# Attention's product with v turned round: queries in rows, the weights' sum as a 65th column, division on VectorE

## The chip, the core and the metric

The kernel runs on one NeuronCore of a Trainium2 chip. Its engines work side by side, each through its own queue in order: TensorE (PE) multiplies matrices, VectorE (DVE), ScalarE (ACT) and GpSimd (POOL) do elementwise work, SyncE (SP) issues the DMA transfers. Matmuls write to PSUM, eight banks of 2 KB per partition. The metric is the device time of one execution in microseconds (us), as the median of three runs.

## What is computed

Causal attention with a decay in the scores (4 batches, 8 heads, 576 positions, 64 columns), then a two-matrix layer with a leaky ReLU (512 to 2048 to 512), then a second layer (512 to 1024, softmax gate, layer norm, back to 512). The change touches only the middle of the attention:

```python
scores = scores - np.max(scores, axis=-1, keepdims=True)
attn = np.exp(scores)
attn = attn / (np.sum(attn, axis=-1, keepdims=True) + 1e-09)
return np.matmul(attn, v).astype(np.float32)
```

## The kernel before

Two heads make a pair, and there are 16 pairs, four to a batch. Queries are cut into blocks of 128 rows; blocks 0 to 3 are whole, block 4 holds the last 64 rows of both heads at once. `pair` (L765) runs one pair. The first four pairs run in two halves: blocks 0 and 1 from a float32 tile `qa` without splitting, later blocks 2 to 4; the other twelve run whole. For each unit of blocks `scores` (L675) lets PE write the scores into PSUM banks `ps_s` (four of them), DVE subtracts the mask and takes the row's extreme (L693), then `softmax` (L636) does the rest: ACT computes exp in place and gives the row's sum as a second output, its accumulator (L643), an engine of choice adds the small guard (L650), DVE takes the reciprocal (L661), ACT or DVE writes the normalised weight's high float16 half to `hl` (L665), DVE the low half (L669), and `turn` (L672) lets a DMA transpose both into `pt`, keys in partitions.

`pv` (L736) then multiplies: the stationary operand is v of 128 keys, split by `prep_v` (L594) into 64 high and 64 low columns side by side in `VT`, and the moving operand is 128 queries of `pt`. High and low half of the weights take one matmul each:

```python
mm(ps.t[:, 128 * i:128 * i + 128], vl(p, hd, j), pts[i][0].t[:, pts[i][1] + k * (i + 1) + j, :],
   j == 0 and k == 0, j == i and k == 1)
```

The output stands with v's columns in partitions, the layout that the next layer wants. Its two halves are added up in `evac` (L721): ACT copies the low one to `xr` (L725), DVE adds the high one (L728). There is one bank `ps_v`. `pv4` (L750) does the same for block 4 with 64 moving columns. `xr` goes out to `xs_d` by DMA, and the FFN reads it back as tokens.

The FFN's first part (`ffn_a`, L875) works in nine blocks of 256 tokens with nine of sixteen chunks of weights; a token block needs the four pairs of its batch. Its matmuls fill PE between attention matmuls. The second part (`ffn_b`, `layer2`) follows.

The order on every engine is not written by hand. `Plan.run` (L163) is a list scheduler: every operation has a priority and an assumed duration, buffers come from tags with a fixed number of tiles, and an operation that may run on several engines (`copy_f`, `sub_f`, `flex`) takes the one that the planner finds cheapest then. Attention comes before FFN on PE. Its constants are the same before and after.

## Time and profile before

| | |
|---|---|
| median of 3 runs | 850.2 us (849.22 to 850.39) |
| the profiled execution's own time | 849.04 us |
| its span in the profile | 847.2 us |
| busy share of the span | PE 92%, DVE 62%, ACT 58%, POOL 43% |
| mean granted clock of PE | 0.98 |
| DMA queue q1 | 105.67 MB, 52.3% of the 16 engines' span |

The span is what the profile shows from the first to the last instruction; the execution's own time has some 2 us more around it. A stretch of the span can have another limit than the whole, so it is read stretch by stretch. "Idle before" in a group of instructions is the time that the engine waited ahead of them, with the releaser.

### The profile page before, as it was taken

The numbers are of one execution on the slowest core, as the hardware profiler recorded it, in microseconds if no ns is written. First come the engines' busy times: TensorE is split into PE (matmuls) and PEld (weight loads), VectorE is DVE, ScalarE is ACT, GpSimd is POOL, SyncE is SP. The second block draws the span as 40 slices with busy tenths as digits, with TensorE's granted clock in tenths as the row PEclk, the third lists the DMA queues.
The fourth block names the chain that finished last, engine by engine and source line by source line (L and its number), as shares of the span: only waits on it lengthen the run. The fifth ranks groups of instructions, "written<-read, shape, count | busy, mean of one in ns | idle before, by whom it ended". The sixth has DMA issues, their size and how long they took to land.

```text
span 847.2 us, 15672 instructions
## 1 busy us (share of the span) xinstructions
PE 777.7 (92%) x5648; PEld 707.1 (83%) x5648; DVE 523.0 (62%) x1301; ACT 488.8 (58%) x1210; POOL 364.5 (43%) x433
## 2 busy tenths in 40 slices
...
GB/s 285 199 231 226 178 142 183 129 185 156 184 137 179 126 197 115 147 165 187 168 175 157 190 26 87 71 68 26 87 38 101 26 88 38 87 26 63 26 42 95
DMA packets 179757, 106.66 MB, mean 126 GB/s; under 512 B 146608, under 2 KB 162496, under 8 KB 179680
## 3 DMA queue, kind: packets, MB, share of 16 engines
q1 hardware_dynamic: 179680, 105.67, 52.3%
q8 instruction: 44, 0.72, 0.4%
...
## 4 chain that ended last, share of the span: by engine, by line
PE 58%; DVE 4%; DMA 3%; ACT 3%; issue 1%; POOL 1%; DVEq 0%; SPq 0%; ACTq 0%; POOLq 0%
PE ps_f L470 36%; PE ph L470 11%; PE py L470 8%; DMA pt<-hl 2%; PE ps_s L470 1%; PE ps_v L470 1%; DMA tr<-hl 1%; ACT hl L424 1%; DVE hl L435 1%; DVE st L657 0%; ACT ps_s L643 0%; DVE g L841 0%; DVE raw L952 0%; DVE ps_s L693 0%; DVE s L944 0%
## 5 line engine op out<-in xcount | busy, mean ns | idle before, releaser
L470 PE MATMUL ps_f<-x,wi 128*128 128x256 f32 x972 | 129.6, 288 | 0.8 <-DVE g L841 0.8
L470 PEld LDWEIGHTS ps_f<-x,wi 128*128 128x128 f32 x972 | 123.6, 193 | 2.0 <-DVE g L841 1.2
L470 PE MATMUL ps_f<-g,wo 128*128 128x256 f32 x972 | 124.2, 283 | 1.2 <-DVE g L841 1.2
L470 PEld LDWEIGHTS ps_f<-g,wo 128*128 128x128 f32 x972 | 119.5, 188 | 1.8 <-DVE g L841 1.5
L470 PE MATMUL ps_s<-kq 128*128 128x512 f32 (+4 forms) x352 | 95.4, 396 | 25.8 <-DVE hl L435 22.4
L470 PE MATMUL ps_f<-x,wib 128*128 128x256 f32 x756 | 98.3, 281 | 0.7 <-DVE g L841 0.4
L470 PEld LDWEIGHTS ps_s<-kq 128*128 128x128 f32 x352 | 65.9, 226 | 39.2 <-DVE hl L435 22.2
L470 PE MATMUL ph<-wi,g 128*128 128x512 f32 x408 | 98.3, 396 | 0.0
L839 ACT ACTIVATE g<-ps_f 128x256 fp32r<-128x256 f32 x144 | 55.2, 383 | 71.9 <-PE ps_f L470 70.8
L470 PEld LDWEIGHTS ps_f<-x,wib 128*128 128x128 f32 x756 | 92.8, 188 | 1.8 <-DVE g L841 1.7
L470 PEld LDWEIGHTS ph<-wi,g 128*128 128x128 f32 x408 | 76.0, 188 | 17.6
L439 POOL TENSOR_TENSOR kq<-raw,kq 64x576 fp32r<-64x576 f32 (+2 forms) x55 | 82.6, 1502 | 14.6 <-ACT kq L424 9.2
L435 DVE SCALAR_TENSOR_TENSOR hl<-ps_s,st,hl 128x512 f16<-128x512 f32 (+4 forms) x160 | 82.2, 538 | 9.1 <-ACT hl L424 7.3
L643 ACT ACTIVATE ps_s<-ps_s,st 128x512 f32<-128x512 f32 (+4 forms) x160 | 78.8, 493 | 13.0 <-DVE st L693 7.7
L841 DVE TENSOR_TENSOR g<-ps_f,g 128x256 fp32r<-128x256 f32 x144 | 60.2, 420 | 41.0 <-ACT ps_f L840 39.3
L470 PE MATMUL ps_f<-wo,x 128*128 128x512 f32 x348 | 83.9, 396 | 0.0
L424 ACT ACTIVATE hl<-ps_s,st 128x512 f16<-128x512 f32 (+4 forms) x146 | 73.0, 538 | 12.3 <-issue 3.2
L470 PEld LDWEIGHTS ps_f<-wo,x 128*128 128x128 f32 x348 | 64.7, 188 | 14.9
L470 PE MATMUL ps_v<-pt,VT 128*128 128x128 f16 (+1 forms) x928 | 65.4, 234 | 12.7 <-DVE xr L728 4.3
L470 PE MATMUL py<-g,wob 128*128 128x256 f32 x567 | 76.6, 279 | 0.0
L470 PEld LDWEIGHTS <-VT 128*128 128x128 f16 x928 | 56.2, 110 | 22.8 <-issue 13.2
L470 PEld LDWEIGHTS py<-g,wob 128*128 128x128 f32 x567 | 72.4, 188 | 1.9
(152 smaller groups left out, 1198.5 us busy)
## 6 DMA issues: line engine op xcount, KB each, us to landing
...
```

Of the source, the lines that this page charges most:

```text
L424: nc.scalar.activation(o, i, CP, scale=1.0 if scale is None else scale)
L435: nc.vector.scalar_tensor_tensor(o, a, scale, b, op0=ALU.mult, op1=ALU.subtract)
L439: (nc.vector if eng == DVE else nc.gpsimd).tensor_tensor(o, a, b, op=ALU.subtract)
L470: nc.tensor.matmul(o, lhsT=l, rhs=r, start=start, stop=stop)
L643: P.op(ACT, act(W, 1, True) + 93, lambda view=view, j=j, k=k: nc.scalar.activation(view(), view(), AF.Exp, bias=sts.t[:, j:j + 1], scale=- ...
L839: P.op(ACT, act(n, 0, True), lambda: nc.scalar.activation(g.t[:, 0, 0:n], h(), AF.Prelu, scale=WSC, alpha=0.01), eprio, w=[(g, 0)], r=[ps])
L841: P.op(DVE, dve(n) + 60, lambda: nc.vector.tensor_tensor(g.t[:, 1, 0:n], h(), g.t[:, 0, 0:n].bitcast(F32), op=ALU.subtract), eprio, w=[(g, ...
```

## The change

The product with v is turned round. `pt` (128 keys by 128 queries) is now the stationary operand and v the moving one, so that a query stands in a row. `VT` holds per block and head 64 low columns, 64 high ones and a column of ones; high columns and ones together are 65 moving columns, and the 65th output column is the sum of the row's weights. A pair of weight halves and v halves takes four matmuls (`pv_mms`), all into the same 65 columns of PSUM, instead of two of 128 columns. The softmax gives no sums any more: exp has no second output, guard and reciprocal are gone, the halves in `hl` are those of exp times the constant 2^15, and blocks 0 and 1 of one bank are split in one pass of 384 columns. The division comes after the product, on DVE: guard and reciprocal of the 65th columns, then one instruction that scales by `u` and the reciprocal into `xn` (`xn4` for block 4, both heads in one matrix with zeros elsewhere). PE turns `xn` back by a float32 matmul with the identity (`across` for blocks 0 to 3, 128 columns a block; inside `pv4` with `ident2`, 64 columns), and ACT or DVE copies the result to `xr`. `xn` lies in the three tiles `sd` that the decay has done with. `prep_v` writes its unused outputs to tiles of their own.

```diff
-    P.tag("VT", tiles(ap, "VT", NVT, [128, 5, 2, 2, 64], F16))
+    P.tag("VT", tiles(ap, "VT", NVT, [128, 5, 2, 130], F16))
+    P.tag("rs", tiles(ap, "rs", 3, [128, 8], F32))
+    P.tag("xn4", tiles(ap, "xn4", 1, [128, 128], F32))
+    vabs = ap.tile([128, 640], F16, name="vabs")
+    vmin = ap.tile([128, 128], F32, name="vmin")
+    ident2 = ap.tile([128, 64], F32, name="ident2")
...
+    heirs("sd", *[lambda t: [("xn", t[:, 0:512].rearrange("p (a b) -> p a b", a=4))]] * 3)
...
+        nc.vector.tensor_tensor(ident2, one_at[:, 0:64], one_at[:, 64:128], op=ALU.add)
+        for v in P.tags["VT"].free:
+            nc.gpsimd.memset(v[:, :, :, 128:129], 1.0)
+        for x in P.tags["xn4"].free:
+            nc.gpsimd.memset(x, 0.0)
...
-        half = lambda l: v.t[:, :, :, l].rearrange("p j h d -> p (j h) d")
+        half = lambda l: v.t[:, :, :, 64 - 64 * l:128 - 64 * l].rearrange("p j h d -> p (j h) d")
...
-                nc.scalar.activation(v.t.rearrange("p j h l d -> p (j h l d)")[:, 0:640], R(), AF.Abs, accum_out=va.t)
...
+                nc.scalar.activation(vabs, R(), AF.Abs, accum_out=va.t)
...
-            v.t.rearrange("p j h l d -> p (j h l d)")[:, 0:256].bitcast(F32), ps.t[:, 0:128], mask[:, 0:128], -1.0, -(2.0 ** -97),
...
+            vmin, ps.t[:, 0:128], mask[:, 0:128], -1.0, -(2.0 ** -97),
...
-    def softmax(parts, prio):
-
-
-        sts, n, nb = parts[0][1], 0, len(parts)
+    def softmax(sts, parts, groups, prio):
...
         hl, pt = P.buf("hl"), P.buf("pt")
-        one = parts[0][2] == parts[-1][2]
-        for k, (view, _, j, W, pieces, ps) in enumerate(parts):
-            P.op(ACT, act(W, 1, True) + 93, lambda view=view, j=j, k=k: nc.scalar.activation(
-                view(), view(), AF.Exp, bias=sts.t[:, j:j + 1], scale=-1.0, accum_out=sts.t[:, 3 + k:4 + k]), prio,
-                w=[(sts, 2)], rw=[ps], r=[(sts, j)])
-
-        ns = 1 if one else nb
-        total, scale = lambda: sts.t[:, 3:3 + ns], lambda: sts.t[:, 6:6 + ns]
-
-        def guard(e):
-            if one and nb == 2:
-                nc.vector.scalar_tensor_tensor(scale(), total(), 1.0e-9, sts.t[:, 4:5], op0=ALU.add, op1=ALU.add)
-                nc.vector.tensor_scalar(scale(), scale(), PS, None, op0=ALU.mult)
-            elif e == ACT:
-                nc.scalar.activation(scale(), total(), CP, scale=PS, bias=1.0e-9 * PS)
-            else:
-                (nc.vector if e == DVE else nc.gpsimd).tensor_scalar(scale(), total(), 1.0e-9, PS, op0=ALU.add, op1=ALU.mult)
-
-        engs = (DVE,) if one and nb == 2 else REC_ENGS
-        flex(engs, [{ACT: 100.0, DVE: 70.0 * nb, POOL: 165.0}[e] for e in engs], guard, prio, w=[(sts, 3)], r=[(sts, 2)])
-        P.op(DVE, 75, lambda: nc.vector.reciprocal(sts.t[:, 9:9 + ns], scale()), prio, w=[(sts, 4)], r=[(sts, 3)])
-        for view, _, j, W, pieces, ps in parts:
-            rs = lambda j=j: sts.t[:, 9 + j:10 + j]
-            for ho, lo, so, w in pieces:
-                copy_f(lambda ho=ho, w=w: hl.t[:, ho:ho + w], lambda so=so, w=w, view=view: view()[:, so:so + w], w, prio,
-                       engs=HI_ENGS, scale=rs, psum=True, w=[(hl, ho)], r=[ps, (sts, 4)])
-            for ho, lo, so, w in pieces:
-                sub_f(lambda lo=lo, w=w: hl.t[:, lo:lo + w], lambda so=so, w=w, view=view: view()[:, so:so + w],
-                      lambda ho=ho, w=w: hl.t[:, ho:ho + w], w, prio, engs=(DVE,), scale=rs,
-                      w=[(hl, lo)], r=[ps, (sts, 4), (hl, ho)])
-                n += 2 * w
+        for view, j, W, ps in parts:
+            P.op(ACT, act(W, 0, True), lambda view=view, j=j: nc.scalar.activation(
+                view(), view(), AF.Exp, bias=sts.t[:, j:j + 1], scale=-1.0), prio, rw=[ps], r=[(sts, j)])
+        n = 0
+        for view, at, W, ps in groups:
+            copy_f(lambda at=at, W=W: hl.t[:, at:at + W], view, W, prio, engs=HI_ENGS, scale=lambda: 1.0 / PS, psum=True, w=[(hl, at)], r=ps)
+            sub_f(lambda at=at, W=W: hl.t[:, at + W:at + 2 * W], view, lambda at=at, W=W: hl.t[:, at:at + W], W, prio, engs=(DVE,),
+                  scale=lambda: 1.0 / PS, w=[(hl, at + W)], r=ps + [(hl, at)])
+            n += 2 * W
         turn(lambda: pt.t[:, 0:n // 128], lambda: hl.t[:, 0:n], n, prio - 500, w=[pt], r=[hl])
         return pt
...
+            parts.append((view, j, W, key))
+            w = 384 if joint else W
+            chunk[i] = (at // 128 + c0 // 128, at // 128 + (c0 + w) // 128)
+            if not joint or i == 1:
+                groups.append((lambda w=w, ps=ps: ps.t[:, 0:w], at, w, [ps]))
+                at += 2 * w
...
+        pt = softmax(sts, parts, groups, prio)
+        return {i: (pt, *c) for i, c in chunk.items()}
...
-    def evac(p, hd, ps, xr, c0, c1, dst0, prio):
-        n = c1 - c0
-        a, b = 64 * hd, 64 * (1 - hd)
-        u = U[p]
-        P.op(ACT, act(n, 1, True), lambda: nc.scalar.activation(
-            xr.t[a:a + 64, dst0:dst0 + n], ps.t[b:b + 64, c0:c1], CP, scale=u.t[b:b + 64]), prio,
-            w=[(xr, (hd, dst0))], r=[ps, u])
-        P.op(DVE, dve(n) + 60, lambda: nc.vector.scalar_tensor_tensor(
-            xr.t[a:a + 64, dst0:dst0 + n], ps.t[a:a + 64, c0:c1], u.t[a:a + 64],
-            xr.t[a:a + 64, dst0:dst0 + n], op0=ALU.mult, op1=ALU.add), prio, rw=[(xr, (hd, dst0))], r=[ps, u])
...
     def vl(p, hd, j):
 
-        return VT[p].t[:, j, hd].rearrange("p l d -> p (l d)")
-
-    def pv(p, hd, pts, xr, prio):
-        ps, blocks = P.buf("ps_v"), sorted(pts)
-        bufs = {id(b): b for b, _ in pts.values()}
...
+        return v[:, 0:64], v[:, 64:129]
+
+    def pv_mms(o, pair, v, first, last):
+
+        h, l = pair
+        vlo, vhi = v
+        mm(o, h, vhi, first, False)
+        mm(o[:, 0:64], h, vlo, False, False)
+        if l is not None:
+            mm(o[:, 0:64], l, vlo, False, False)
+            mm(o, l, vhi, False, last)
+
+    def pv(p, hd, pts, xn, prio):
+        ps, rs, blocks = P.buf("ps_v"), P.buf("rs"), sorted(pts)
...
+        def pe():
+            for n, i in enumerate(blocks):
+                pt, h, l = pts[i]
+                for j in range(i + 1):
+                    pv_mms(ps.t[:, 65 * n:65 * n + 65], (pt.t[:, h + j], pt.t[:, l + j]), vl(p, hd, j), j == 0, j == i)
+
+        P.op(PE, sum(4 * (i + 1) * mmh(65) for i in blocks), pe, prio, w=[ps], r=[VT[p]] + list(bufs.values()))
+        o = lambda a, b: ps.t[:, 0:65 * nb].rearrange("p (n d) -> p n d", d=65)[:, :, a:b]
+        P.op(DVE, 70, lambda: nc.vector.tensor_scalar(rs.t[:, 0:nb].unsqueeze(2), o(64, 65), 1.0e-9 / PS, None, op0=ALU.add), prio, w=[(rs, 0)], r=[ps])
+        P.op(DVE, 75, lambda: nc.vector.reciprocal(rs.t[:, 4:4 + nb], rs.t[:, 0:nb]), prio, w=[(rs, 1)], r=[(rs, 0)])
+        P.op(DVE, dve(64 * nb) + 60, lambda: nc.vector.scalar_tensor_tensor(
+            xn.t[:, b0 % 4:b0 % 4 + nb, 64 * hd:64 * hd + 64], o(0, 64), U[p].t, rs.t[:, 4:4 + nb].unsqueeze(2).to_broadcast([128, nb, 64]),
+            op0=ALU.mult, op1=ALU.mult), prio, w=[(xn, hd)], r=[ps, (rs, 1), U[p]])
...
+    def pv4(p, pt, xr, prio):
+
+        ps, rs, xn = P.buf("ps_v"), P.buf("rs"), P.buf("xn4")
+
+        def pe():
+            for hd in range(2):
+                o = ps.t[:, 65 * hd:65 * hd + 65]
+                for j in range(4):
+                    pv_mms(o, (pt.t[:, j], pt.t[:, 4 + j]), vl(p, hd, j), j == 0, False)
+                vlo, vhi = vl(p, hd, 4)
+                mm(o[:, 0:64], pt.t[:, 8], vlo, False, False)
+                mm(o, pt.t[:, 8], vhi, False, True)
+
+        P.op(PE, 36 * mmh(65), pe, prio, w=[ps], r=[VT[p], pt])
+        own = [slice(64 * hd, 64 * hd + 64) for hd in range(2)]
+        for hd, a in enumerate(own):
+            P.op(DVE, 70, lambda hd=hd, a=a: nc.vector.tensor_scalar(
+                rs.t[a, 0:1], ps.t[a, 65 * hd + 64:65 * hd + 65], 1.0e-9 / PS, None, op0=ALU.add), prio, w=[(rs, hd)], r=[ps])
+        P.op(DVE, 75, lambda: nc.vector.reciprocal(rs.t[:, 4:5], rs.t[:, 0:1]), prio, w=[(rs, 2)], r=[(rs, 0), (rs, 1)])
+        for hd, a in enumerate(own):
+            P.op(DVE, dve(64) + 60, lambda hd=hd, a=a: nc.vector.tensor_scalar(
+                xn.t[a, a], ps.t[a, 65 * hd:65 * hd + 64], U[p].t[a], rs.t[a, 4:5], op0=ALU.mult, op1=ALU.mult), prio, w=[(xn, hd)], r=[ps, (rs, 2), U[p]])
+        P.op(PE, 107.0, lambda: mm(ps.t[:, 256:320], xn.t, ident2, True, True), prio, rw=[ps], r=[xn], heat=HEAT)
+        copy_f(lambda: xr.t[:, 512:S], lambda: ps.t[:, 256:320], 64, prio, engs=HI_ENGS, psum=True, w=[(xr, 1)], r=[ps])
...
+    def across(p, xn, blocks, xr, prio):
...
         def pe():
             for i in blocks:
-                for j in range(i + 1):
-                    for k in range(2):
-                        mm(ps.t[:, 128 * i:128 * i + 128], vl(p, hd, j), pts[i][0].t[:, pts[i][1] + k * (i + 1) + j, :],
-                           j == 0 and k == 0, j == i and k == 1)
-
-        P.op(PE, sum(2 * (i + 1) * mmh(128) for i in blocks), pe, prio, w=[ps], r=[VT[p]] + list(bufs.values()))
-        evac(p, hd, ps, xr, 128 * blocks[0], 128 * (blocks[-1] + 1), 128 * blocks[0], prio)
...
+                mm(ps.t[:, at(i)], xn.t[:, i], ident.bitcast(F32), True, True)
+
+        P.op(PE, len(blocks) * 215.0, pe, prio, w=[ps], r=[xn], heat=HEAT)
+        a, b = 128 * blocks[0], 128 * blocks[-1] + 128
+        copy_f(lambda: xr.t[:, a:b], lambda: ps.t[:, a:b], b - a, prio, engs=HI_ENGS, psum=True, w=[(xr, 0)], r=[ps])
...
-            pv(p, hd, pts, xr, prio + AV)
+            pv(p, hd, pts, xn, prio + AV)
...
+        across(p, xn, [i for i in blocks if i < 4], xr, prio + AV)
```

In numbers of instructions on PE: 928 products with v become 1856, each with its load of weights, and 64 transposes of 128 and 16 of 64 columns are added. 88 DMA transposes are issued before and after, and SP's queue holds 364 rows both times.

First place, PE, the end of a product with v in one of the first pairs (`VT` is v, `pt` the transposed weights, `sd` a tile that holds `xn`). Before:

```order
L470 LDWEIGHTS VT_106
L470 MATMUL ps_v_164<-pt_131,VT_106 128x128
L470 LDWEIGHTS VT_106
L470 MATMUL ps_v_164<-pt_131,VT_106 128x128
L470 MATMUL ps_s_161<-kq_0_144 128x384
L470 MATMUL ps_s_161<-kq_1_145 128x384
```

Now:

```order
L477 LDWEIGHTS pt_136
L477 MATMUL ps_v_171<-VT_105,pt_136 128x64
L477 LDWEIGHTS pt_136
L477 MATMUL ps_v_171<-VT_105,pt_136 128x64
L477 LDWEIGHTS pt_136
L477 MATMUL ps_v_171<-VT_105,pt_136 128x65
L477 MATMUL ps_s_170<-qa 128x256
L477 MATMUL ps_f_163<-ident,va_142 128x128
L477 MATMUL ps_s_168<-kq_0_151 128x384
L477 MATMUL ps_s_168<-kq_1_152 128x384
L477 MATMUL ps_v_171<-ident,sd_124 128x128 x2
```

Loads come from `pt`, the matmuls are 65 and 64 columns wide, and the turn back stands four matmuls later, behind the DVE work that it needs.

Second place, DVE, within a whole pair (`st` holds row statistics, `rs` the sums and reciprocals; an `ISA` row is the masked extreme or the reading of its result). Before:

```order
L693 ISA st_124 128x1
L435 SCALAR_TENSOR_TENSOR hl_126<-ps_s_161,st_123,hl_126 128x512
L661 RECIPROCAL st_119<-st_119 128x1
L693 ISA ps_s_162,st_124<-ps_s_162,mask 128x384
L693 ISA st_124 128x1
L427 CAST kq_1_141<-kq_0_140 64x640
L435 SCALAR_TENSOR_TENSOR hl_127<-ps_s_160,st_119,hl_127 128x512
L693 ISA ps_s_161,st_121<-ps_s_161,mask 128x512
L693 ISA st_121 128x1
L728 SCALAR_TENSOR_TENSOR xr_132<-ps_v_164,u_110,xr_132 64x512
```

Now:

```order
L687 ISA ps_s_169,st_131<-ps_s_169,mask 128x384
L687 ISA st_131 128x1
L687 ISA ps_s_168,st_128<-ps_s_168,mask 128x512
L687 ISA st_128 128x1
L741 TENSOR_SCALAR rs_110<-ps_v_171 128x4
L687 ISA ps_s_167,st_131<-ps_s_167,mask 128x256
L687 ISA st_131 128x1
L742 RECIPROCAL rs_110<-rs_110 128x4
L442 SCALAR_TENSOR_TENSOR hl_132<-ps_s_169,hl_132 128x384
L743 SCALAR_TENSOR_TENSOR sd_124<-ps_v_171,u_116,rs_110 128x4x64
```

The reciprocal ahead of the low half is gone; three instructions after the product take the place of the merge on L728, with other work between them.

Third place, PE, where FFN blocks fill it (`g`, `wo` are the FFN's operands):

```order
L477 MATMUL ps_f_163<-g_906,wo_72 128x256 x3
L477 MATMUL ps_f_163<-g_907,wo_73 128x256 x3
L477 MATMUL ps_f_163<-g_908,wo_74 128x256 x3
L477 MATMUL ps_f_163<-g_909,wo_75 128x256 x3
L477 MATMUL ps_v_171<-ident,sd_123 128x128 x2
L477 MATMUL ps_f_162<-g_906,wo_72 128x256 x3
L477 MATMUL ps_f_162<-g_907,wo_73 128x256 x3
L477 MATMUL ps_f_162<-g_908,wo_74 128x256 x3
L477 MATMUL ps_f_162<-g_909,wo_75 128x256 x3
L477 LDWEIGHTS pt_136
```

The turn back has twelve matmuls of the FFN ahead of it, between it and the product; before there was no such step.

## Rows read from the trace of the kernel before

**Rows 1.** The page, busy time, share of the span and instructions of each engine.
```profile
PE 777.7 (92%) x5648; PEld 707.1 (83%) x5648; DVE 523.0 (62%) x1301; ACT 488.8 (58%) x1210; POOL 364.5 (43%) x433
```

**Rows 2.** Busy time (instructions) by stretch: PE, weight loads, DVE, ACT, POOL, granted clock, DMA.
```profile
core 0: us, PE busy (x) PEld busy (x) DVE busy (x) ACT busy (x) POOL busy (x), PEclk, DMA share, GB/s
0.00:98.00 98.00, 53.77 (x269) 39.74 (x269) 85.64 (x232) 77.74 (x183) 78.78 (x94) 1.00 0.87 228
98.00:183.00 85.00, 82.52 (x744) 79.12 (x744) 71.14 (x223) 76.39 (x207) 52.06 (x50) 0.96 0.78 159
183.00:219.00 36.00, 24.52 (x168) 20.46 (x168) 29.87 (x91) 26.55 (x71) 21.30 (x22) 0.68 0.79 168
219.00:368.00 149.00, 143.90 (x1342) 137.08 (x1342) 118.32 (x360) 127.69 (x357) 71.39 (x76) 0.98 0.74 148
368.00:847.00 479.00, 472.96 (x3133) 430.67 (x3132) 218.06 (x399) 180.44 (x396) 140.97 (x194) 1.00 0.33 89
```

**Rows 3.** Timeline of PE, 80 to 125 us: start, length, group of instructions.
```profile
84.04 1.65 PE L470 MATMUL ps_v<-pt,VT 128*128 128x128 f16 x14 [0.71 <-ACT hl L424]
85.45 0.99 PE L470 MATMUL ps_s<-kq 128*128 128x384 f32 x2
...
98.08 2.91 PE L470 MATMUL ps_f<-x,wi 128*128 128x256 f32 x12
```

**Rows 4.** Timeline of PE around 219 and 368 us.
```profile
219.05 0.77 PE L470 MATMUL ps_f<-x,wi 128*128 128x256 f32 x2
...
367.84 10.32 PE L470 MATMUL ps_f<-g,wo 128*128 128x256 f32 x84
```

**Rows 5.** Waits of PE, 183 to 219 us: us in total, times, longest.
```profile
PE ps_s L470 <- DVE hl L435: 8.6, 3, 3.8
PE ps_v L470 <- DVE xr L728: 1.8, 1, 1.8
```

**Rows 6.** Timeline of PE, 250 to 262 us: products with v and what follows.
```profile
252.55 1.29 PE L470 MATMUL ps_v<-pt,VT 128*128 128x128 f16 x20
253.65 0.89 PE L470 MATMUL ps_s<-kq 128*128 128x512 f32 x4
...
258.55 0.70 PE L470 MATMUL ps_v<-pt,VT 128*128 128x64 f16 x18 [0.86 <-DMA pt<-hl]
259.08 2.04 PE L470 MATMUL ps_f<-g,wo 128*128 128x256 f32 x15
```

**Rows 7.** Records of one tile, 32.0 to 33.2 us: min/median/max ns, first and last start.
```profile
L470 PE MATMUL ps_s<-qa x4: 634/634/635, 31.7 to 33.0; 66*128 66x256 f32 x4
```

**Rows 8.** Groups by line: weight loads for the products with v; busy us, mean ns.
```profile
L470 PEld LDWEIGHTS <-VT 128*128 128x128 f16 x928 | 56.2, 110 | 22.8 <-issue 13.2 <-DMA pt<-hl 3.9 <-DVE st L693 2.3
```

**Rows 9.** Groups by line and form on DVE and ACT.
```profile
L728 DVE SCALAR_TENSOR_TENSOR xr<-ps_v,u,xr 64x64 f32<-64x64 f32 (+2 forms) x72 | 34.7, 482 | 8.3 <-ACT xr L725 7.0
...
L725 ACT ACTIVATE xr<-ps_v,u 64x64 f32<-64x64 f32 (+2 forms) x72 | 33.8, 470 | 10.5 <-PE ps_v L470 6.4 <-DVE xr L728 2.7
L643 ACT ACTIVATION_READ_ACCUMULATOR ps_s<-ps_s,st 128x1 f32 x160 | 32.4, 203 | 0.2
...
L661 DVE RECIPROCAL st<-st 128x1 f32<-128x1 f32 (+2 forms) x88 | 14.2, 163 | 10.5 <-POOL st L657 6.7 <-ACT st L655 2.4
...
L1000 ACT ACTIVATE ot<-ps_f 128x512 f32<-128x512 f32 x18 | 10.8, 597 | 59.7 <-PE ps_f L470 54.7 <-issue 5.0
...
L652 DVE SCALAR_TENSOR_TENSOR st<-st 128x1 f32<-128x1 f32 x16 | 10.3, 642 | 0.5 <-ACT ps_s L643 0.3
...
L657 DVE TENSOR_SCALAR st<-st 128x1 f32<-128x1 f32 (+2 forms) x18 | 7.4, 410 | 1.7 <-ACT ps_s L643 1.5
...
L424 ACT ACTIVATE hl<-ps_s,st 128x512 f16<-128x512 f32 x48 | 32.9, 685 | 7.6 <-issue 3.2 <-DVE st L661 2.5 <-ACT hl L424 1.0
```

**Rows 10.** Busy time by stretches of 10 us; the DMA share is the last but one.
```profile
20.00:30.00 10.00, 4.49 (x16) 2.63 (x14) 9.13 (x33) 8.31 (x27) 9.42 (x12) 1.00 0.72 197
...
40.00:50.00 10.00, 7.57 (x37) 5.54 (x36) 9.07 (x31) 9.26 (x25) 7.28 (x11) 1.00 0.96 238
...
60.00:70.00 10.00, 7.26 (x48) 5.53 (x48) 9.27 (x26) 9.02 (x23) 7.70 (x8) 1.00 1.11 225
```

50 lines of the change are left out of this document (18 added, 32 removed).

## The prediction

> **What bounds the kernel now.** The page first: TensorE (PE) is busy 92% of the span [rows 1]. An average over stretches with different limits says little, so I cut the span at PE's own events and read the busy time by stretch [rows 2]. The cuts are the first FFN matmul at 98.08 us [rows 3], the first FFN matmul of token block 2 at 219.05 and the end of the last attention matmul at 367.84 [rows 4]; 183 is where FFN blocks 0 and 1 run out. The reader should see three kinds of time in the five rows. From 98 to 183, from 219 to 368 and from 368 on PE is full (97 to 99%): a us of PE work added there costs a us. Up to 98 PE is busy 53.8 of 98 us and waits for others, DVE at 87% and the DMA engines at 0.87. From 183 to 219 it is busy 24.5 of 36 us at a granted clock of 0.68: the FFN has no tokens left until batch 1 is through attention. PE waits there for PSUM banks that the softmax holds, 8.6 us on the low halves written by DVE [rows 5].
>
> So attention work on PE is free in two stretches and paid in three, while DVE and ScalarE (ACT) work on attention is paid in those two stretches and nearly free elsewhere. The change moves work from DVE and ACT to PE. Both signs are in it.
>
> **PE work added.** Twenty 128-column products with v take 253.65 - 252.55 = 1.10 us, 55 ns each; eighteen 64-column ones take 259.08 - 258.55 = 0.53 us, 29.4 ns each, weight load included [rows 6]. Blocks 0 to 3: 640 matmuls of 128 columns become 1280 of 64 or 65, 35.2 to 37.6 us, +2.4. Block 4: 288 of 64 columns become 576, because both heads' 128 rows are now multiplied with both heads' v, 8.5 to 16.9 us, +8.4. The turn back: 64 float32 transposes of 128 columns and 16 of 64. The float32 products of the first pairs leave a 256-column record every (33.0 - 31.7) / 3 = 0.43 us [rows 7], and one matmul of the code is two such records (32 stand for 16), so 128 columns took about 0.43 us there. That was at a slow pace: 14 products with v of 128 columns took 85.45 - 84.04 = 1.41 us, 101 ns each [rows 3], against 55 later. At the later pace a transpose is 0.43 x 55 / 101 = 0.23 us. The bounds are 0.1 (half of that again) and 0.43; I take 0.22, since PE was full and fast wherever it is paid. That gives 64 x 0.22 + 16 x 0.11 = 15.8. Sum: 2.4 + 8.4 + 15.8 = 26.6 us.
>
> How much is paid? Pricing the order of both kernels matmul by matmul at these paces, attention ahead of the first FFN matmul goes from 25.1 to 27.7 us: 2.6 fall into the first stretch, where PE waits anyway. The other **24 us** lie behind it.
>
> Against a small price of the doubled weight loads stands a row: their records last 110 ns each [rows 8], and 928 more would be 102 us if they queued. They do not, since load and 64-column matmul together pass in 29.4 ns. The Trainium skill (TensorE: Matmul & The Clock Gate, LDWEIGHTS) gives columns / 1.2 ns, an estimate of 107 ns for 128 columns; by it the sum would be about +99 instead of +24, and the 29.4 ns of this trace disagree.
>
> **Vector work removed.** DVE loses the 72 evacuations that merge halves (34.7 us), 88 reciprocals (14.2), the doubled guard of block 4 (10.3) and its share of the other guards (7.4): 66.6 [rows 9]. It gains 40 normalising evacuations (at the 0.482 mean of the old ones, 19.3), 56 reciprocals (0.163, 9.1), 72 one-column guards from PSUM (at a reciprocal's 0.163, 11.7; bounds 0.1 and 0.3) and 32 of 64 columns (0.16 to 0.48; I take 0.2, 6.4): 46. Net -20 us, 1.3 us a pair of heads. Joining two passes of hi and lo in every joint unit is left uncounted, on the gaining side. ACT loses 72 evacuations (33.8) and 160 accumulator reads, 32.4 of records that overlap their activation; I take half, 16, with 0 and 32 as bounds. A constant scale costs less than one from a column, 597 against 685 ns for 512 columns, 0.09 x 124 hi copies = 11. It gains 34 copies of turned results, about 13. Net -48 us, 3 us a pair [rows 9]. POOL loses its guards.
>
> **Start of the FFN, 98 us.** The first FFN block waits for the 18 weight chunks and four pairs' first rows. The order puts 27.7 / 8.8 = 3.1 pairs of attention ahead of it instead of 25.1 / 7.2 = 3.5 (8.8 and 7.2 us of PE work a pair). DVE saves 0.35 x 15 + 3.1 x 1.3 = 9 us of its 85.6. But the DMA engines ran at 0.96 to 1.11 from 40 to 70 us and only at 0.72 from 20 to 30 [rows 10], and the chunks come through them. So not all of it shows: I take **-6** (bounds 0 and -12, the last when nothing of the DMA binds).
>
> **The gap, 183 to 219.** Before, the order has 14.3 us of attention between the last matmul of FFN block 1 and the first of block 2, two pairs, in 36 us: 18.1 us a pair and 21.7 us lost. Now it has 11.3 us, 1.28 pairs. DVE, the busiest there (29.9 of 36, 15.0 us a pair), falls by 9%, so a pair takes 18.1 x 0.91 = 16.5 us and the gap 21. Lost: 21 - 11.3 = 9.7, **-12**. The price of the new chain is in it: a bank of products is now freed by three DVE instructions in a row (guard, reciprocal, evacuation), block 4 also by a transpose and a copy, and PE's queue behind waits. There is one such bank.
>
> **From 219 on.** 219 to 368 contains some 12 us beyond the 137 of priced work, partly again waits for tokens; with attention further ahead I take **-6** (0 to -8). FFN work left after the last attention matmul grows from 464.5 to 486.5 us, only because attention ends earlier; this is the same 24 us of displacement and not counted twice. DMA transposes are the same 88, SP's queue has the same rows in another order.
>
> **Sum.** +24 - 6 - 12 - 6 = 0 us. The profiled execution's own time is 849.04, the median of the runs 850.2; on the median I forecast **851 us**, a wash with the terms read upward by one for waits on the single bank.
>
> **The rivals.**
> 1. *Faster: the vector engines were the real limit.* If the start moves by the full 12 us and the gap's loss nearly closes (-18) with -7 later, the sum is 24 - 37 = -13, 838 us. For it: every serial step of the softmax between scores and DMA transpose gets shorter, and guard and reciprocal (two hops) leave the chain. Against: the DMA rows. Chance 0.28.
> 2. *Slower: the gap does not close.* In the gap PE ran at half clock for much of the time (0.68), and attention costs 8.8 us of PE per pair at full clock, 17.6 at half. If the clock stays low, PE is what a pair waits for: 1.28 x 17.6 = 22.5 us and 3 us of waits on the bank, and the DMA engines (0.79 busy there) hold the start. Then -1 at the start, -7 in the gap, -1 later: +15, 866 us. It decides if less than 24 us of idle time are recovered. Chance 0.22.
> 3. *Slower: long bursts of small matmuls do not hold 29.4 ns.* The trace shows 18 in a row; now 36 and 40 come in a row, each with its load. At 40 ns (between 29.4 and the 55 of a 128-column one) 1856 x 10.6 ns = 19.7 us, four fifths paid: +16, 867 us. Chance 0.08.
> 4. *Weight loads in a row*, the rule above as a mechanism of this kernel: 928 more at the 110 ns of their records, +102 us, 950. The 29.4 ns speak against it. Chance 0.02.
>
> That the change does not do what it says is not a rival: the order shows the guards gone and the transposes there.
>
> **How the numbers follow.** The forecast (844 to 858) has 0.40. About 0.2% of the time, 1.7 us, is what a measurement can tell from no change. Of the forecast's 0.40 I give 0.12 to faster, 0.16 to same, 0.12 to slower. Faster: 0.28 + 0.12 = 0.40. Same: 0.16. Slower: 0.12 + 0.22 + 0.08 + 0.02 = 0.44. The range takes in rivals 1 and 2, 838 to 867, and leaves the ends beyond them out; the forecast's own range is 844 to 858.
>
> **What would show it.** Right: products with v at 29 ns a matmul; float32 transposes near 0.22 us; first FFN matmul near 92, the gap near 21 us, the last attention matmul near 346 to 350, and the rest as full as now. Wrong in the gaining direction: the first FFN matmul before 88 and no gap left. Wrong in the other: PE waiting for the bank of products on DVE's evacuation in the full stretches, a granted clock below 0.7 over a gap of 30 us, or product bursts at 40 ns.

## The result, and the profile after

The changed kernel takes **855.38 us** (median of 4 runs, 854.64 to 857.04), the one before, on the same chip, 850.09 us (849.22 to 850.39): a ratio of **1.0067, 95% interval 1.0049 to 1.0084**. It is slower by 5.3 us by the medians, by 0.67% as the ratio gives it. Forecast were 851 us with a range of 838 to 867. The profiled execution took 854.84 us, its span is 853.1 us, where it was 847.2.

The page and the stretches, cut at the same events as in [rows 2]: first FFN matmul, end of FFN block 1, first matmul of block 2, last attention matmul.

```profile
PE 796.4 (93%) x6736; PEld 731.5 (86%) x6736; DVE 484.5 (57%) x1252; ACT 442.8 (52%) x982; POOL 343.7 (40%) x392
```

```profile
core 0: us, PE busy (x) PEld busy (x) DVE busy (x) ACT busy (x) POOL busy (x), PEclk, DMA share, GB/s
0.00:97.70 97.70, 56.92 (x402) 45.31 (x403) 76.74 (x221) 69.20 (x135) 74.29 (x84) 0.92 0.93 230
97.70:199.70 102.00, 100.82 (x1215) 96.84 (x1214) 79.68 (x266) 77.49 (x176) 61.68 (x52) 0.97 0.77 162
199.70:220.00 20.30, 15.30 (x203) 12.47 (x201) 14.87 (x55) 15.93 (x35) 12.06 (x12) 0.92 0.92 208
220.00:351.00 131.00, 127.68 (x1602) 123.22 (x1601) 94.80 (x310) 91.95 (x221) 58.76 (x53) 1.00 0.76 155
351.00:853.00 502.00, 495.68 (x3324) 453.63 (x3323) 218.44 (x404) 188.25 (x418) 136.88 (x193) 1.00 0.32 86
```

The vector engines are busy 38 us (DVE) and 46 us (ACT) less than in [rows 1]. The gap shrank from 36.0 to 20.3 us and its granted clock rose from 0.68 to 0.92. Attention ends 17 us earlier and leaves 23 us more of FFN behind it. But the first stretch is nearly as long as before, 97.7 us for 98.1.

The start of the FFN in PE's timeline (start, length, group, idle time before it):

```profile
36.46 1.22 PE L477 MATMUL ps_v<-ident,sd 128*128 128x128 f32 x4 [0.51 <-DVE vs L626]
37.34 2.05 PE L477 MATMUL ps_s<-kq 128*128 128x512 f32 x4
...
46.37 1.22 PE L477 MATMUL ps_v<-ident,sd 128*128 128x128 f32 x4 [3.68 <-DVE sd L743]
...
76.29 0.69 PE L477 MATMUL ps_v<-ident,xn 128*128 128x64 f32 x2 [3.84 <-DVE xn L767]
...
93.68 1.69 PE L477 MATMUL ps_v<-VT,pt 128*128 128x65 f16 x28 [1.40 <-ACT xr L431]
95.18 2.75 PE L477 MATMUL ps_s<-kq 128*128 128x512 f32 x8
97.74 1.63 PE L477 MATMUL ps_f<-x,wi 128*128 128x256 f32 x6
```

The first two rows show PE's pace here: two turns (4 records, since a float32 matmul of the code is two) take 37.34 - 36.46 = 0.88 us, 0.44 each.

What PE waited for in 0 to 98 us, first before, then after (us in total, times, longest):

```profile
PE ps_s L470 <- DVE hl L435: 16.1, 10, 3.9
PE ps_f L470 <- DMA qa<-sd: 15.6, 1, 15.6
PE ps_v L470 <- DVE xr L728: 2.5, 3, 1.4
PE ps_v L470 <- DVE vs L614: 2.2, 1, 2.2
...
PE ps_f L470 <- ACT VT L605: 0.6, 1, 0.6
```

```profile
PE ps_f L477 <- ACT vabs L617: 17.6, 2, 16.6
PE ps_s L477 <- DVE hl L442: 10.0, 7, 2.3
PE ps_v L477 <- DVE sd L743: 6.9, 5, 3.7
PE ps_v L477 <- DVE xn L767: 3.8, 1, 3.8
PE ps_v L477 <- ACT xr L431: 1.7, 2, 1.4
```

All rows for `ps_s` together fell from 19.6 to 10.0 us: the shorter softmax frees the score banks sooner. All rows for `ps_v` rose from 8.3 to 12.9 us: PE now stands at turns, whose input VectorE writes after guard and reciprocal. The rows for `ps_f` rose from 16.2 to 17.6 us, 1.0 of it because the first loads came later in this execution (first PE instruction at 16.6 us, before at 15.6). PE itself is busy 3.1 us longer. -9.6 + 4.6 + 1.4 + 3.1 = -0.5, and the FFN started 0.4 us earlier; the rest is in gaps too short for the list. The busy time by itself, from the first score matmul to the first FFN matmul, before and after:

```profile
15.90:98.10 82.20, 53.57 (x270) 39.54 (x269) 74.43 (x215) 70.08 (x171) 67.97 (x73) 0.99 0.88 223
```

```profile
16.90:97.70 80.80, 56.64 (x402) 45.04 (x403) 66.99 (x203) 61.54 (x123) 63.42 (x58) 0.91 0.94 228
```

Busy 53.6 and 56.6 us, waiting 28.6 and 24.2.

PE in a full stretch, with products in a row and turns:

```profile
240.75 1.05 PE L477 MATMUL ps_v<-ident,sd 128*128 128x128 f32 x8
241.56 1.77 PE L477 MATMUL ps_s<-kq 128*128 128x256 f32 x8
243.16 1.39 PE L477 MATMUL ps_v<-VT,pt 128*128 128x65 f16 x40
244.38 0.61 PE L477 MATMUL ps_s<-kq 128*128 128x64 f32 x4
...
252.04 0.33 PE L477 MATMUL ps_v<-ident,xn 128*128 128x64 f32 x2
252.18 0.89 PE L477 MATMUL ps_s<-kq 128*128 128x512 f32 x4
```

Forty products take 244.38 - 243.16 = 1.22 us, 30.5 ns each, weight load included. Four turns of 128 columns (8 records) take 241.56 - 240.75 = 0.81 us, 0.20 each, half of what one takes ahead of the FFN; one of 64 columns takes 0.14. At these prices the turns are 64 x 0.20 + 16 x 0.14 = 15.0 us in all.

So the account of the 5.9 us of span, with the same price for each form of matmul in both kernels, "lost" being what a stretch is longer than its priced work:

| | predicted | before | after | difference |
|---|---|---|---|---|
| first FFN matmul | -6 | 98.1 | 97.7 | -0.4 |
| attention's PE work behind it | +24 | 87.9 | 111.5 | +23.6 |
| lost from there to block 2 (gap included) | -12 | 31.0 | 17.5 | -13.5 |
| lost from block 2 to the last attention matmul | -6 | 14.7 | 10.0 | -4.7 |
| lost behind that | 0 | 20.2 | 21.2 | +1.0 |

The +23.6 can be redone from the matmuls that changed, those behind the first FFN matmul. Before, 522 products of 128 columns at 55 ns and 234 of 64 at 29.4 ns are 35.6 us. Now 1576 products at 29.4 ns, 54 turns at 0.20 us and 14 at 0.14 are 59.1 us: +23.5. At the 30.5 ns of this trace it would be 1.7 more, and the lost time 1.7 less. The split of the lost time over its rows rests on the prices of all forms and is an estimate.

### The profile page after: what moved, and what is told of

Its sections match the earlier page's. It is cut to its first block, busy times and chain, and to the rows that moved or that the text cites. A ratio compares the mean times of both kernels' runs of the same rounds, so it can differ in the third digit from the quotient of the medians.

```text
span 853.1 us, 17526 instructions
## 1 busy us (share of the span) xinstructions
PE 796.4 (93%) x6736; PEld 731.5 (86%) x6736; DVE 484.5 (57%) x1252; ACT 442.8 (52%) x982; POOL 343.7 (40%) x392
## 4 chain that ended last, share of the span: by engine, by line
PE 79%; DMA 8%; DVE 5%; ACT 4%; issue 2%; SPq 1%; POOL 1%; ACTq 0%; DVEq 0%
PE ps_f L477 47%; PE ph L477 11%; PE py L477 8%; PE ps_v L477 7%; PE ps_s L477 6%; DMA pt<-hl 5%; DMA vr<-vt 2%; DMA tr<-hl 1%; ACT ps_s L654 1%; ACT hl L431 1%; SPq L468 1%; DVE wst L819 1%; DVE hl L442 1%; DVE ps_s L687 1%; ACT kq L431 1%
## 5 line engine op out<-in xcount | busy, mean ns | idle before, releaser
L860 ACT ACTIVATE g<-ps_f 128x256 fp32r<-128x256 f32 x144 | 55.2, 383 | 91.1 <-PE ps_f L477 90.1
L477 PE MATMUL ps_s<-kq 128*128 128x512 f32 (+4 forms) x352 | 89.4, 377 | 8.7 <-DVE hl L442 7.5
L446 POOL TENSOR_TENSOR kq<-raw,kq 64x576 fp32r<-64x576 f32 (+2 forms) x52 | 78.3, 1507 | 33.0 <-ACT kq L431 30.3
L477 PEld LDWEIGHTS ph<-wi,g 128*128 128x128 f32 x408 | 76.0, 188 | 17.6
L654 ACT ACTIVATE ps_s<-ps_s,st 128x512 f32<-128x512 f32 (+4 forms) x160 | 76.3, 495 | 21.6 <-DVE st L687 12.8
L442 DVE SCALAR_TENSOR_TENSOR hl<-ps_s,hl 128x384 f16<-128x384 f32 (+2 forms) x128 | 70.1, 560 | 26.1 <-ACT hl L431 24.8
L477 PEld LDWEIGHTS <-pt 128*128 128x128 f16 x1856 | 66.9, 102 | 16.0 <-issue 13.9
L477 PE MATMUL ps_v<-VT,pt 128*128 128x65 f16 (+1 forms) x1856 | 72.5, 200 | 6.7 <-ACT xr L431 3.7
L477 PEld LDWEIGHTS ps_s<-kq 128*128 128x128 f32 x352 | 60.5, 212 | 15.8 <-DVE hl L442 8.7
L687 DVE CUSTOM_DVE_ANT_0 ps_s<-ps_s,mask 128x512 f32<-128x512 f32 (+3 forms) x128 | 62.2, 499 | 11.8 <-PE ps_s L477 6.7
```

The costliest lines, as they stand in the source:

```text
L442: nc.vector.scalar_tensor_tensor(o, a, scale, b, op0=ALU.mult, op1=ALU.subtract)
L446: (nc.vector if eng == DVE else nc.gpsimd).tensor_tensor(o, a, b, op=ALU.subtract)
L477: nc.tensor.matmul(o, lhsT=l, rhs=r, start=start, stop=stop)
L654: P.op(ACT, act(W, 0, True), lambda view=view, j=j: nc.scalar.activation(view(), view(), AF.Exp, bias=sts.t[:, j:j + 1], scale=-1.0), prio ...
L687: P.op(DVE, dve(W) + 130, lambda i=i, j=j, view=view: nc.vector.tensor_tensor_reduce(view(), view(), mask[:, 384 - 128 * i:512], -0.125, 3 ...
L860: P.op(ACT, act(n, 0, True), lambda: nc.scalar.activation(g.t[:, 0, 0:n], h(), AF.Prelu, scale=WSC, alpha=0.01), eprio, w=[(g, 0)], r=[ps])
```

## The experiments

All times are compared with runs of the kernel before on the same chip, as ratios. By these the changed kernel is at 1.0067. The table gives the times in the profiled execution of each run: the first score matmul (it moves with the first loads, from 15.4 to 17.6 us without any edit ahead of it), the first FFN matmul, the time between these two, the gap ahead of block 2 and the end. Two things limit what the table can tell. By the ratios e3, e4 and e12 each lie some 3 us from the changed kernel, with an uncertainty of 2.4 to 3 us by their intervals. And the columns of times come from one execution of each run: with the same 401 matmuls between first scores and first FFN matmul, PE was busy 55.2 us there in e7 and 56.6 in the changed kernel, so that a difference of less than 1.5 us in "between" cannot be put down to an edit.

| run | ratio, interval | first scores | first FFN | between | gap | end |
|---|---|---|---|---|---|---|
| before | 1 | 15.9 | 98.1 | 82.2 | 36.0 | 847.2 |
| after | 1.0067 (1.0049 to 1.0084) | 16.9 | 97.7 | 80.8 | 20.3 | 853.1 |
| e1 | 0.9825 (0.9799 to 0.9851) | 16.0 | 93.0 | 77.0 | 30.7 | 835.0 |
| e2 | 0.9936 (0.9917 to 0.9954) | 16.6 | 95.3 | 78.8 | 18.9 | 842.2 |
| e3 | 1.0030 (1.0008 to 1.0051) | 15.8 | 95.0 | 79.2 | 20.5 | 848.0 |
| e4 | 1.0103 (1.0073 to 1.0134) | 17.6 | 100.3 | 82.7 | 20.5 | 858.2 |
| e5 | 1.1453 (1.1420 to 1.1486) | 16.6 | 85.9 | 69.3 | 66.8 | 972.6 |
| e6 | 1.0222 (1.0194 to 1.0250) | 17.4 | 101.0 | 83.6 | 37.6 | 866.9 |
| e7 | 1.0110 (1.0077 to 1.0144) | 19.4 | 99.7 | 80.3 | 20.4 | 859.3 |
| e8 | 1.0055 (1.0023 to 1.0086) | 16.0 | 95.5 | 79.5 | 16.6 | 852.6 |
| e9 | 1.0222 (1.0177 to 1.0268) | 15.5 | 94.6 | 79.1 | 29.8 | 868.6 |
| e10 | 1.0138 (1.0111 to 1.0166) | 15.4 | 98.8 | 83.3 | 24.4 | 853.0 |
| e11 | 0.9947 (0.9928 to 0.9966) | 17.1 | 97.2 | 80.1 | 25.3 | 842.6 |
| e12 | 1.0032 (1.0005 to 1.0058) | 15.7 | 94.7 | 78.9 | 20.0 | 850.4 |

**e1 to e4: one part of the change at a time.** In all four the planner was told the old durations, so that the order of the work stayed.

e1, the lighter softmax alone, in the kernel before. Shown are two of its four places; guard and reciprocal issue nothing either. The evacuations that merge halves and the separate passes of blocks 0 and 1 stay, and nothing is added in place of the division:

```diff
-  view(), view(), AF.Exp, bias=sts.t[:, j:j + 1], scale=-1.0, accum_out=sts.t[:, 3 + k:4 + k]), prio,
+  view(), view(), AF.Exp, bias=sts.t[:, j:j + 1], scale=-1.0), prio,
...
-  rs = lambda j=j: sts.t[:, 9 + j:10 + j]
+  rs = lambda: 1.0 / PS
```

> The kernel before with the order of every engine kept, but exp gives no sums, guard and reciprocal issue nothing and the weights are scaled by a constant (the output is left without the division). Theory A (PE is full outside two stretches, so vector work counts only in those): the first FFN matmul stays near 98 us because the DMA engines bring it, the gap of 36 us shrinks to 29 to 32, in all -4 to -8 us against before. Rival B (the vector engines set the pace of attention everywhere): about -20 us.

Measured: 834.85 us, 1.75% under before, 14.9 us by the ratio, between the two. The FFN starts 5.2 us earlier, counted from the first scores, and the gap shrinks by 5.3. Its time from the first scores to the first FFN matmul:

```profile
16.00:93.00 77.00, 53.91 (x269) 39.46 (x269) 66.00 (x177) 64.19 (x135) 66.77 (x62) 0.90 0.95 236
```

PE waits 77.0 - 53.9 = 23.1 us there, before 28.6. So the forecast's -6 was near what the lighter softmax is worth at the start when nothing is added.

e2, the low by low products (448 of 1856) left out, a term of about 2 to the power -22 of a product:

```diff
-            mm(o[:, 0:64], l, vlo, False, False)
```

> The changed kernel without the 448 products of low half with low half, durations given to the planner unchanged, so the order stands. Theory A: 448 x 29.4 ns = 13.2 us less on PE, some 80 to 90% of it paid, so -10 to -12 us against the changed kernel (about 844). Rival C (the added products lie beside waits on the one product bank and on DVE): 0 to -3 us.

Measured: 844.04 us, 0.9936, against 1.0067 of the changed kernel 11.1 us less. At 30.5 ns the 448 products are 13.7 us, so four fifths of this PE work were paid, 2.0 us of it at the start. **This kernel beats both.** The saving needs the new orientation, as the layout suggests; no run of the old one without this term was made. Before, high and low half of v are columns of one stationary tile, and one product with 128 moving columns [rows 6] makes both.

e3, the turn as float16 (the result's precision falls with it):

```diff
-    P.tag("xn4", tiles(ap, "xn4", 1, [128, 128], F32))
+    P.tag("xn4", tiles(ap, "xn4", 1, [128, 128], F16))
...
-                mm(ps.t[:, at(i)], xn.t[:, i], ident.bitcast(F32), True, True)
+                mm(ps.t[:, at(i)], xn.t[:, i], ident3, True, True)
```

> The changed kernel with the turn back as float16 matmuls instead of float32 (the turned result keeps 11 bits), order kept. Theory A: 64 x (0.224 - 0.056) + 16 x (0.112 - 0.029) = 12.1 us less on PE, so -9 to -11 us against the changed kernel (about 845). Rival C (the turn waits for DVE's evacuation, its own length is hidden): 0 to -3 us.

Measured: 852.54 us, by the ratios 3.1 us under the changed kernel: a miss for the theory that the turn is paid nearly in full, and at the edge of rival C's range. Its timeline shows four turns in 236.28 - 236.08 = 0.20 us:

```profile
236.08 0.40 PE L478 MATMUL ps_v<-ident,sd 128*128 128x128 f16 x4
236.28 1.55 PE L478 MATMUL ps_s<-kq 128*128 128x256 f32 x7
```

Per turn that is a quarter of the float32 price; 16 x 0.6 + 16 x 0.1 = 11 us of PE work are gone. In the profiled execution 1.6 us came back at the start (PE busy 2.1 us less, waits 0.5 more) and 2.4 behind it:

```profile
15.80:95.00 79.20, 54.57 (x391) 41.94 (x390) 68.36 (x203) 61.14 (x122) 63.19 (x58) 0.89 0.93 230
```

The rest was taken up by other losses. Part of them can be seen: one burst of 36 products and one of 40 stood in a stretch with half the granted clock, 54 to 56 ns a product in place of 30.5, where the changed kernel had one burst of 40 so, and PE waited behind two other bursts for 1.6 and 1.5 us, where the changed kernel had one such wait of 1.2. In the gap the granted clock was 0.75, where it had been 0.92:

```profile
211.32 2.35 PE L478 MATMUL ps_v<-VT,pt 128*128 128x65 f16 x40 [0.81 <-DVE xr L435]
213.47 1.72 PE L478 MATMUL ps_s<-kq 128*128 128x384 f32 x6
```

```profile
194.80:215.10 20.30, 16.24 (x195) 13.37 (x195) 14.59 (x54) 14.87 (x33) 11.65 (x12) 0.75 1.01 226
```

Where the other 4 us or so went was not settled.

e4, the accumulator output back in exp, unused:

```diff
-  view(), view(), AF.Exp, bias=sts.t[:, j:j + 1], scale=-1.0), prio, rw=[ps], r=[(sts, j)])
+  view(), view(), AF.Exp, bias=sts.t[:, j:j + 1], scale=-1.0, accum_out=sts.t[:, 4 + j:5 + j]), prio, rw=[ps], r=[(sts, j)])
```

> The changed kernel with the accumulator output of exp put back, unused, order kept: 160 reads of about 0.1 us beyond their activation, 16 us of ACT. Theory A: 0 to +2 us against the changed kernel, all of it ahead of the first FFN matmul or in the gap. Rival B: +6 to +16 us.

Measured: 858.32 us, 3.1 us over the changed kernel by the ratios, somewhat above theory A's 2. 1.9 us of it stand at the start, and the gap does not move, although its granted clock was 1.00, where the changed kernel's was 0.92. ACT is busy 459.2 us after 442.8: of 160 records of 201 ns, 32.1 us, half lies beside the exp, as the prediction took it.

```profile
PE 795.4 (93%) x6736; PEld 729.3 (85%) x6736; DVE 485.6 (57%) x1252; ACT 459.2 (54%) x1142; POOL 343.3 (40%) x392
```

```profile
202.70:223.00 20.30, 13.93 (x201) 11.07 (x200) 14.93 (x55) 16.87 (x46) 11.69 (x12) 1.00 0.94 199
```

**e5 to e8: what holds the start.** Candidates were the one product bank, TensorE's queue, and the DMA engines. e5:

```diff
-        ps = P.buf("ps_v")
+        ps = P.buf("ps_s")
         at = lambda i: slice(128 * i, 128 * i + 128)
```

> The turn of the four blocks writes to one of the four score banks in place of the one product bank, so that the next products wait for VectorE's division alone and not for the turn and its copy; the planner writes a new order, in which only 233 matmuls stand ahead of the first FFN matmul, where there were 649. Theory Q (the FFN starts at 97.7 us because TensorE's queue holds attention work ahead of it, part of it waiting for the one product bank): first FFN matmul at 92 to 95 us, waits on the product bank ahead of it under 6 us where they were 12.9, time 848 to 853 us. Rival D (x, through the DMA queues, is what is late; they are 0.93 busy there): first FFN matmul at 96 to 98 us, time 854 to 857 us.

Measured: 973.59 us, a miss for both. The planner hands out the banks of a pool in the order in which the code asks for them, and the turn asks after all of its own pair's scores. So no score of the next pair could take a bank ahead of the turn: exactly 24 score matmuls stand between any two later turns of the order, where the changed kernel's has 6 to 32. PE's timeline shows the chain of one pair laid bare:

```profile
158.85 1.71 PE L477 MATMUL ps_v<-VT,pt 128*128 128x65 f16 x28 [4.77 <-DMA pt<-hl]
162.49 2.15 PE L477 MATMUL ps_v<-VT,pt 128*128 128x65 f16 x36 [1.93 <-DMA pt<-hl]
165.99 0.69 PE L477 MATMUL ps_v<-ident,xn 128*128 128x64 f32 x2 [1.36 <-DVE xn L767]
166.99 1.69 PE L477 MATMUL ps_v<-VT,pt 128*128 128x65 f16 x28 [0.31 <-ACT xr L431]
169.59 1.23 PE L477 MATMUL ps_s<-ident,sd 128*128 128x128 f32 x4 [0.91 <-DVE sd L743]
170.47 5.16 PE L477 MATMUL ps_s<-kq 128*128 128x512 f32 x16
```

It tells nothing on the start of the changed kernel, but what it costs when pairs hardly overlap: by the ratios 118 us. e6:

```diff
-    P.tag("ps_s", tiles(ps_a, "ps_s", 4, [128, 512], F32))
-    P.tag("ps_v", tiles(ps_a, "ps_v", 1, [128, 512], F32))
+    P.tag("ps_s", tiles(ps_a, "ps_s", 3, [128, 512], F32))
+    P.tag("ps_v", tiles(ps_a, "ps_v", 2, [128, 512], F32))
```

> Two product banks and three score banks, where there were one and four; the planner writes a new order. Theory Q, with the product bank as the scarce one: waits on it ahead of the first FFN matmul under 6 us where they were 12.9, first FFN matmul at 94 to 96.5 us, time 849 to 854 us. Rival W (the score banks are the scarce ones, since each is held through mask, exp and split): waits on ps_s go up from 10 us to over 15 in their place, time 856 to 862 us.

Measured: 868.69 us, slower than either theory had it. Waits on `ps_v` in 0 to 98 us rose from 12.9 to 18.5 us with twice the banks; most of them stand at turns, whose data VectorE has not written:

```profile
PE ps_v L477 <- DVE sd L743: 14.4, 5, 6.6
PE ps_s L477 <- DVE hl L442: 6.5, 6, 2.0
PE ps_v L477 <- DMA pt<-hl: 2.9, 2, 2.0
```

So a second product bank, bought with a score bank, did not remove these waits. Rival W's own sign, longer waits on `ps_s`, did not show either, and the gap, 37.6 us, is where most of the time went. e7:

```diff
-        load(s, lambda: half(1025, I16)[:, 1:2049], lambda: src.bitcast(I16), 524288, prio - LDW if lead is None else lead)
+        n = 1024 if stage[0] == "wst" else 2048
+        load(s, lambda: half(1025, I16)[:, 1:n + 1], lambda: src.bitcast(I16)[:, 0:n], 524288, prio - LDW if lead is None else lead)
```

> Half of each chunk of FFN weights that goes through the wst tiles is not loaded (it stays zero, the output is not the reference's): 17 transfers of 512 KB become 256 KB, all ahead of the FFN or beside it. TensorE's, VectorE's and ScalarE's orders are those of the changed kernel. Rival D (DMA is the floor under the start of the FFN): first FFN matmul at 92 us or earlier, time 851 us or less. Theory Q: first FFN matmul at 96.5 to 98 us, time 853 to 856 us.

Measured: 858.99 us, outside both ranges. The zeroing of three tiles on POOL, which the expectation had not priced, put the first scores 2.5 us later. From there to the first FFN matmul it is 80.3 us, after 80.8, with the DMA share down from 0.93 to 0.73:

```profile
0.00:99.70 99.70, 55.64 (x402) 43.92 (x403) 77.40 (x221) 68.98 (x135) 77.25 (x87) 0.94 0.73 180
```

The bytes of the weights are not the floor. e8:

```diff
-        gs = [hidden(c, xb, TB, "ps_f", "g", prio + c, eprio + c) for c in range(FA)]
+        gs = [hidden(c, xb, TB, "ps_f", "g", 0.0 if blk == 0 and c < 3 else prio + c, eprio + c) for c in range(FA)]
```

> The first three chunks of FFN block 0 get a priority ahead of the attention's; in the order, four score matmuls of 512 columns (2.6 us at the lower clock) go from ahead of the first FFN matmul to behind it. Theory Q: first FFN matmul at 94.5 to 95.5 us, and the time 852 to 856 us, since work is only moved. Rival D (x is late): first FFN matmul at 97 to 98 us with a wait for x ahead of it.

Measured: 855.12 us, 1.0055 with an interval that takes in 1.0067. The first FFN matmul came at 95.5 us, straight behind the scores and without a wait for x, so PE's queue did hold it; 1.3 us of the 2.2 remain when it is counted from the first scores. The time did not follow: work was only moved.

**e9 to e12: the chain from products to turn.** e9 has the planner count 2 us more ahead of a turn:

```diff
-            op0=ALU.mult, op1=ALU.mult), prio, w=[(xn, hd)], r=[ps, (rs, 1), U[p]])
+            op0=ALU.mult, op1=ALU.mult), prio, w=[(xn, hd)], r=[ps, (rs, 1), U[p]]).lag = 2000.0
...
+        P.tags["ps_v"].fifo = False
```

> The planner counts 2 us more between VectorE's division and the turn that reads it, so that it puts other work of TensorE in between, and it may give the product bank to the next products ahead of the turn; the work is the same. Theory T (ahead of the first FFN matmul TensorE stands at turns whose data VectorE has not yet written, 9.9 us of its 12.9 us of waits on ps_v there, and the order is what makes it stand): these waits fall under 5 us, first FFN matmul at 93 to 96 us, time 848 to 853 us. Rival V (the chain through VectorE and ScalarE is what is late, whatever stands at the head of TensorE's queue): the waits go to score banks and products, first FFN matmul at 96 to 99 us, time 854 to 858 us.

Measured: 869.38 us, far above both ranges. The first FFN matmul, at 94.6 us, lies where theory T had it, but T's reason falls: the turns stopped waiting for VectorE, but products took the wait over, 10.3 us for VectorE's scaling, where it had been 6.9 and 3.8. One place in the timeline and the row of the waits:

```profile
46.43 0.81 PE L477 MATMUL ps_v<-VT,pt 128*128 128x65 f16 x12 [5.13 <-DVE sd L743]
```

```profile
PE ps_v L477 <- DVE sd L743: 10.3, 4, 5.1
```

Attention as a whole fell behind: it ended at 379.6 us in place of 351.1, and the gap grew to 29.8 us. e10 is the same on e2, with the planner told of three products:

> The same as in e9, on the kernel that leaves out the low by low products (a term of about 2 to the power -22 of a product), with the planner told that there are three products and not four. If theory T holds: 839 to 843 us, faster than the 844.04 of the three products alone. Rival V: 843 to 847 us.

Measured: 860.12 us, slower than e2 by 2%, like e9, and outside both ranges. e11 is e2 with the planner's price of the products changed (one of two lines):

```diff
-        P.op(PE, sum(4 * (i + 1) * mmh(65) for i in blocks), pe, prio, w=[ps], r=[VT[p]] + list(bufs.values()))
+        P.op(PE, sum(3 * (i + 1) * mmh(65) for i in blocks), pe, prio, w=[ps], r=[VT[p]] + list(bufs.values()))
```

> Three products, and the planner told so; nothing else. It tells what a new order alone is worth: 842 to 846 us if the order follows the work (844.04 with the old order), above 848 us if an order made by the planner's durations is a matter of luck of some us.

Measured: 844.80 us, no different from e2: this new order is worth nothing. e12 takes guard and reciprocal out of the chain (128 instructions by the profile; the expectation said 112). One of its lines is shown; the scaling, which no longer reads the reciprocal, takes 477 ns after 478 for four blocks and 280 after 342 for block 4:

```diff
-  P.op(DVE, 75, lambda: nc.vector.reciprocal(rs.t[:, 4:4 + nb], rs.t[:, 0:nb]), prio, w=[(rs, 1)], r=[(rs, 0)])
+  P.op(DVE, 75, lambda: None, prio, w=[(rs, 1)], r=[(rs, 0)])
```

> VectorE no longer adds the guard nor takes the reciprocal between the products with v and the turn, 112 instructions in all; it only scales the products by the column u (the output stays undivided), and the orders of the engines are otherwise those of the changed kernel. Theory V (ahead of the first FFN matmul the chain through VectorE is what is late: softmax, then guard, reciprocal and scaling with TensorE waiting at the turn or for the product bank): waits on ps_v for VectorE there fall from 11.2 us to 8 or less, first FFN matmul at 94.5 to 96.5 us, time 849.5 to 853 us. Rival P (TensorE's added work at half pace fills the stretch and VectorE's chain is beside it): first FFN matmul at 97 to 98.5 us, time 854 to 856.5 us.

Measured: 852.35 us, 3.0 us less by the ratios. The same turn as above now waits 2.34 us in place of 3.68, and waits on `ps_v` for VectorE are 8.6 us after 11.2:

```profile
43.80 1.22 PE L477 MATMUL ps_v<-ident,sd 128*128 128x128 f32 x4 [2.34 <-DVE sd L743]
...
94.66 2.91 PE L477 MATMUL ps_f<-x,wi 128*128 128x256 f32 x12
```

The first FFN matmul comes 3.0 us earlier, 1.2 of it with the first loads and 1.9 behind them. Time and first FFN matmul lie in theory V's ranges, the waits for VectorE somewhat above its 8. But the 1.9 us are not mainly waits:

```profile
15.70:94.70 79.00, 55.46 (x402) 43.90 (x402) 63.48 (x173) 62.10 (x123) 65.01 (x57) 0.96 0.95 235
```

Against the changed kernel PE waits 23.5 us in place of 24.2. Of the 2.6 us less for VectorE, 2.0 came back as waits for score banks (10.0 to 10.8 for `hl`) and for ScalarE's copies (1.7 to 2.8). The other 1.2 us are PE's busy time for the same 401 matmuls, at a granted clock of 0.96 for 0.91. The 3.8 us at the turn of block 4 are as before, so guard and reciprocal are not what that turn waits for.

## Why the prediction was off by 4 us

**PE work added, 26.6 us, 24 of them paid: the price held.** Products at 29.4 ns were 30.5; the turn, taken at 0.22 and 0.11 us, was 0.20 and 0.14 in the full stretches. By e2 four fifths of the products left out came back as time. e3 adds a limit: 11 us of turns taken out gave back 3. So added PE work and lost time are not independent terms; that other engines catch up while PE turns, and that PE meets their waits without the turn, is a reading that no run shows. The +23.6 is what the rows price, not what undoing it would return.

**Vector work removed: VectorE's term was too small.** The forecast was -20 us for it and -48 for ACT; measured are -38.5 and -46.0. Of the 18.5 us between, 12.1 are the low halves (82.2 to 70.1 us), whose joined passes the prediction left uncounted.

**The gap, -12: right in size (-13.5; 20.3 us for 21), with a reason that the runs support only in part.** In the order of before, lighter vector work did shorten it (e1, 36.0 to 30.7). In the new order it does not respond: putting 16 us of ScalarE's work back (e4) or taking 128 VectorE instructions out (e12) leaves it at 20.5 and 20.0. Nor does it respond to the granted clock: the gap is 20.5 us at 0.75 (e3) and at 1.00 (e4). VectorE is busy 73% of it now, after 83%. Of the 15.7 us that the gap lost, 9.2 are PE's busy time (24.5 to 15.3), although the priced work fell by 3.0 only; PE went through its work faster, at a granted clock of 0.92 for 0.68. The prediction's step from 36 to 21 had no term for that, and whether the clock shortened the gap or the shorter gap raised the clock is not shown. What is left of the prediction's reason is the order, in which 1.28 pairs of attention stand in the gap, where there were two; what limits it now was not settled.

**From 219 on, -6: near** (-4.7, and 1.0 lost behind the last attention matmul).

**Start of the FFN, -6: this step failed.** It measured -0.4, or -1.4 counted from the first scores. The step took VectorE's saving, cut it for the DMA engines, and counted the 2.6 us of PE work ahead of the FFN as free "where PE waits anyway". The runs put this in its place. Counted from the first scores PE waited 4.5 us less and was busy 3.1 us more: what was saved is in the waits, and the added work was paid on top. PE is slow over much of this stretch: each of the first turns takes 0.44 us there, where the step counted the 0.22 of the full stretches. Lighter softmax alone is worth -5.2, all of it in the waits (e1). The float32 turns cost 1.6 of it again: e3 takes 2.1 us of busy time out, and the waits grow by only 0.5. Guard and reciprocal between products and turn cost 0.6 in waits (e12). -5.2 + 1.6 + 0.6 = -3.0 against the -1.4 measured. The other 1.6 us stay open; they are about what PE's busy time for the same matmuls differs by between executions, and the parts were measured in two kernels with two orders. The mistake was to read PE's idle time up to 98 us as room. PE works through one queue in order, and there attention is a chain: scores, softmax, DMA transpose, products, VectorE, turn, copy. Work put into the chain lengthens it even where its engine idles; for PE's turns e3 shows it, for VectorE's division e12 shows 0.6 us. The DMA rows [rows 10] that the step set against VectorE did not bind as far as the weights go (e7).

**The rivals.** Rival 1 is refuted: with vector work lighter still (e12) the start moved by 1.9 at most, not by 12. Rival 2 was right in the sign and wrong in its mechanism: the gap did close, at a granted clock of 0.92, and at 0.75 in e3. Rival 3 is refuted by bursts of 36 and 40 at 30.5 ns in the full stretches. Rival 4 as well: the Trainium skill (TensorE: Matmul & The Clock Gate, LDWEIGHTS) gives an estimate of 107 ns for a load of 128 columns, and the loads' records do last 102 ns on average, but load and product together pass in 30.5 ns.
